# Layernorm statistics with tokens on the partitions, two layernorms in one call, and reordered loads

## The chip, the cores and the metric

The kernel runs on one core of a Trainium2 chip. The metric is the device time of one execution in microseconds (us). Engines are named as in the profile: PE is TensorE (PEld its weight loads), DVE is VectorE, ACT is ScalarE, POOL is GpSimd, SP is SyncE, which issues most DMAs.

## The reference

```python
def _A_ref(q, k, v, shift_k, ssm_k, ssm_D):      # q = layernorm(x), S = 2048 tokens, D = 512
    k_pad = jnp.pad(k, ((0, 0), (ks - 1, 0), (0, 0)))
    for t in range(ks):                          # ks = 4
        k_shift = k_shift + k_pad[:, t:t + S, :] * shift_k[:, ks - 1 - t][None, None, :]
    kv = k_shift * v
    kv_f = rfft(kv padded to 2 * S);  kf_f = rfft(ssm_k padded to 2 * S)
    y = irfft(kv_f * kf_f)[:S] + kv * ssm_D
    return q * y

def _B_ref(x, w1, w2, w3, w4):
    h = _gelu(_layernorm(x) @ w1)
    # four groups of channels, shifted by +1, -1, +2, -2 tokens
    hs = jnp.concatenate([g0, g1, g2, g3], axis=-1) @ w2
    x1 = x + hs
    return x1 + _gelu(_layernorm(x1) @ w3) @ w4  # w3: 512 x 1792

x = A_q
h = x + _A_ref(_layernorm(x), A_k, A_v, A_shift_k, A_ssm_k, A_ssm_D)
return h + _B_ref(_layernorm(h), B_w1, B_w2, B_w3, B_w4)
```

## The kernel before

Activations lie transposed: channels on the 128 partitions, in 4 chunks, and the 2048 tokens along the free side, mostly worked on in 4 windows of 512 (a block is 128 tokens). A tile scheduler takes the program in the order in which it is written and sets the order within each engine by its own rules; each engine and each DMA queue then works through its list in order.

The stages:

- Start: constants. `bj` (L71 to L74) and `rv` feed the angles of the transforms; `ssk` (L79 to L81) holds the shift weights. `xT` is A_q, transposed by four DMAs on SP (L95). They wait for the scaling of `bj` (L74), since the space of a temporary pool above it is used again.
- `layernorm_feat(xT, qnT, "qn")` (L156). The helper (L116 to L154) squares the whole input (`sq`, L122) and then goes window by window: 8 matmuls of 512 columns with `ones_col` as the stationary operand make sums in one row of one partition (L127, L129); mean, variance, square root, reciprocal and `brow` are computed on that row of 512 (L136 to L142); two f32 matmuls spread the rows over 128 partitions (`psbc`, L145, L146); two ScalarE copies make `abc` and `bbc` (L149, L150); 8 VectorE steps apply them (L153, L154).
- K and V: `kT` by transposing DMAs on SP (L170), `vT` on ScalarE's queue (L172). VectorE makes the shifted sum `ksh` (L175, L177) and the product `kvTc` (L181) of each chunk; TensorE transposes it block by block (L184) into `kv_all`, copied out by ScalarE and VectorE in turn (L187, L189). `hf`, the long filter, comes by 16 transposing DMAs on SP (L192).
- The transforms: a forward one over 17 strips (L202 to L261) and an inverse one over 4 windows (L273 to L295), by matmuls with sines and cosines that `gen_trig` makes on VectorE and ScalarE. Its last steps write `hT` (L294).
- `layernorm_feat(hT, hnT, "hn")` (L319), and `layernorm_feat(hnT, hnnT, "hnn")` (L331), which normalizes the result once more; mixer with `w1` and `w2` (L335 to L352), whose result is `x1T`.
- `layernorm_feat(x1T, ln1T, "ln1")` (L357); the last two matmuls with `w3` and `w4` and a gelu between them (L365 to L390). The weights `w3` and `w1` are loaded on SP's queue, `w4` and `w2` on ScalarE's.

`gelu_psum` (L298 to L308) starts with a ScalarE copy out of PSUM into `xs` (L300).

## Time and profile before

| | us |
|---|---|
| median of five runs | 839.98 (836.65 to 840.39) |
| profiled execution, its own time | 835.66 |
| its span | 833.9 |
| PE busy | 611.9 (73%) |
| DVE busy | 585.6 (70%) |
| ACT busy | 384.8 (46%) |
| PE weight loads busy | 249.9 (30%) |

The span runs from the first to the last instruction of the profiled execution; its own time lies 1.8 us above it. Busy shares are means over stages that are limited by different engines, so the sections below go by stage. In the profile's rows `L122` is line 122 of the kernel, `out<-in` names the tiles, `x4` counts instructions, and a bracket gives the idle time before a row and what released it.

### The profile page before, as it was taken

Reading aid. Unit: us, or ns where it says so; the run is one execution under the profiler, and the core shown is the slowest. Engines: PE = TensorE matmul, PEld = TensorE weight load, DVE = VectorE, ACT = ScalarE, POOL = GpSimd, SP = SyncE. Lnnn points to the kernel's source line nnn. Section 1 sums busy time; section 2 is a strip of 40 time slices with the busy share of each in tenths; the row PEclk is TensorE's granted clock in tenths of the full one; section 3 lists DMA queues with packets and bytes.
Section 4 is the critical chain, followed back from the end, with each engine's and each line's share of the span. In section 5 each row is a group of like instructions: output and inputs, shape, how many; then the busy total and the mean of one; then the engine's idle time right before and its main releaser. Section 6 shows DMA issues by size and latency. Waiting matters only on the chain.

```text
span 833.9 us, 6601 instructions
## 1 busy us (share of the span) xinstructions
PE 611.9 (73%) x2434; PEld 249.9 (30%) x2480; DVE 585.6 (70%) x882; ACT 384.8 (46%) x470; POOL 3.8 (0%) x10
## 2 busy tenths in 40 slices
PE   1550248999999999928999985657457456889885
PEld 0110113444444444403444431111123112334332
DVE  3886694747767666189999828978557894767665
ACT  0110136365564646258787721101392116786771
POOL 1000000000000000000000000000000000000000
PEclk9855558999999999978999995555699758999998
DMA  5006530000000000000000005010000000000000
GB/s 101 0 0 125 105 73 0 1 1 1 0 1 1 1 0 1 1 1 1 0 1 1 1 0 176 0 51 0 0 1 1 0 0 1 0 26 26 0 26 25
DMA packets 39921, 15.62 MB, mean 19 GB/s; under 512 B 34513, under 2 KB 39378, under 8 KB 39890
## 3 DMA queue, kind: packets, MB, share of 16 engines
q1 hardware_dynamic: 29234, 10.76, 5.4%
q10 hardware_dynamic: 10656, 4.46, 2.1%
q8 instruction: 19, 0.31, 0.2%
q14 instruction: 12, 0.10, 0.0%
HBM read 4.72 MB, written 2.10 MB: 8 GB/s over the span
## 4 chain that ended last, share of the span: by engine, by line
PE 52%; DVE 26%; ACT 13%; DMA 4%; issue 2%; SPq 1%; POOL 0%; ACTq 0%; DVEq 0%; POOLq 0%
PE yps L283 7%; PE yps L285 6%; PE ghi L222 6%; PE ghr L220 6%; DVE rows L141 6%; PE aki L221 6%; PE akr L219 6%; ACT xs L300 4%; PE po L378 4%; DVE u L305 3%; PE psbc L146 3%; DVE sq L122 2%; ACT u L302 2%; DMA kT<-in_A_k_dram 2%; ACT sg L307 2%
## 5 line engine op out<-in xcount | busy, mean ns | idle before, releaser
L283 PE MATMUL yps<-ics,Qr 128*128 128x512 bf16 x256 | 98.4, 384 | 18.6 <-ACT ics L114 17.8
L108 DVE TENSOR_TENSOR e<-bj,rv 128x2048 f32<-128x2048 f32 (+2 forms) x34 | 75.7, 2226 | 47.8 <-ACT cs L114 43.2
L222 PE MATMUL ghi<-hf,ss 128*128 128x512 bf16 x256 | 98.0, 383 | 0.7 <-issue 0.2
L220 PE MATMUL ghr<-hf,cs 128*128 128x512 bf16 x256 | 97.0, 379 | 0.5
L221 PE MATMUL aki<-kv_all,ss 128*128 128x512 bf16 x245 | 93.8, 383 | 1.3 <-ACT kv_all L187 1.3
L285 PE MATMUL yps<-iss,Qi 128*128 128x512 bf16 x245 | 93.9, 383 | 0.0
L219 PE MATMUL akr<-kv_all,cs 128*128 128x512 bf16 x246 | 93.3, 379 | 0.4 <-ACT cs L114 0.4
L113 ACT ACTIVATE e<-t 128x2048 f32<-128x2048 f32 (+2 forms) x34 | 63.0, 1852 | 49.2 <-DVE t L111 48.8
L378 PE MATMUL po<-g_sb,w_sb 128*128 128x512 bf16 x217 | 62.3, 385 | 23.8 <-DVE g_sb L308 21.8
L111 DVE TENSOR_TENSOR t<-e,t 128x2048 f32<-128x2048 f32 (+2 forms) x34 | 75.8, 2228 | 1.0
L145 PE MATMUL psbc<-rows,ones_row 1*128 1x512 f32 x32 | 28.4, 983 | 49.8 <-DVE rows L141 49.8
L141 DVE RECIPROCAL rows<-rows 1x512 f32<-1x512 f32 x16 | 53.4, 3335 | 5.0 <-ACT rows L140 5.0
L371 PE MATMUL pg<-ln1T,w_sb 128*128 128x512 bf16 x220 | 55.6, 387 | 1.6 <-ACT bbc L150 1.2
L140 ACT ACTIVATE rows<-rows,eps_t 1x512 f32<-1x512 f32 x16 | 11.5, 719 | 97.2 <-DVE rows L139 97.2
L307 ACT ACTIVATE sg<-u 128x512 bf16<-128x512 bf16 x72 | 44.9, 628 | 17.9 <-DVE u L305 16.7
L184 PE MATMUL pt<-ident,kvTc 128*128 128x128 bf16 x64 | 14.4, 269 | 50.5 <-DVE kvTc L181 24.1
L112 ACT ACTIVATE ss<-t 128x2048 bf16<-128x2048 f32 (+1 forms) x17 | 31.1, 1831 | 37.7 <-DVE t L111 37.6
L129 PE MATMUL stt<-sq,ones_col 128*1 128x512 bf16 x64 | 34.8, 582 | 16.7 <-DVE sq L122 16.7
L303 DVE TENSOR_SCALAR u<-u 128x512 bf16<-128x512 bf16 x72 | 20.5, 290 | 37.2 <-ACT u L302 36.2
L302 ACT ACTIVATE u<-xs 128x512 bf16<-128x512 bf16 x72 | 42.0, 626 | 0.3
L109 DVE TENSOR_SCALAR t<-e 128x2048 f32<-128x2048 f32 (+2 forms) x34 | 40.6, 1194 | 1.9
L114 ACT ACTIVATE ics<-e,halfpi 128x2048 bf16<-128x2048 f32 x16 | 32.0, 2002 | 20.8 <-PE yps L283 20.7
(108 smaller groups left out, 909.5 us busy)
## 6 DMA issues: line engine op xcount, KB each, us to landing
out_dram<-osb SPq DMA_DIRECT2D x16, 128.0 KB, 1.8
w_sb<-in_B_w_dram ACTq DMA_DIRECT2D x1, 1792.0 KB, 12.6
w_sb<-in_B_w_dram SPq DMA_DIRECT2D x1, 1792.0 KB, 8.7
w_sb<-in_B_w_dram ACTq DMA_DIRECT2D x1, 512.0 KB, 5.5
w_sb<-in_B_w_dram SPq DMA_DIRECT2D x1, 512.0 KB
hf<-in_A_ssm_k_dram SPq DMA_TRANSPOSE x16, 2.8
xT<-in_A_q_dram SPq DMA_TRANSPOSE x4, 5.1
kT<-in_A_k_dram SPq DMA_TRANSPOSE x4, 4.1
```

Of the source, the lines that this page charges most:

```text
L108: nc.vector.tensor_tensor(out=ev, in0=bj_b, in1=rv_b, op=MUL)
L111: nc.vector.tensor_tensor(out=tv, in0=ev, in1=tv, op=SUB)
L113: nc.scalar.activation(ev, tv, ACT.Abs)
L141: nc.vector.reciprocal(rstd, varr)
L219: nc.tensor.matmul(akr[:], lhsT=lhs_c, rhs=kv_all[:, b, :], start=st, stop=sp)
L220: nc.tensor.matmul(ghr[:], lhsT=lhs_c, rhs=hf[:, b, :], start=st, stop=sp)
L221: nc.tensor.matmul(aki[:], lhsT=lhs_s, rhs=kv_all[:, b, :], start=st, stop=sp)
L222: nc.tensor.matmul(ghi[:], lhsT=lhs_s, rhs=hf[:, b, :], start=st, stop=sp)
L283: nc.tensor.matmul(yps[:, c, :], lhsT=Qr[:, q, c * P:(c + 1) * P], rhs=ics[:, qi, :], start=(q == 0), stop=False)
L285: nc.tensor.matmul(yps[:, c, :], lhsT=Qi[:, q, c * P:(c + 1) * P], rhs=iss[:, qi, :], start=False, stop=False)
L307: nc.scalar.activation(sg[:], u[:], ACT.Sigmoid)
L378: nc.tensor.matmul(po[:], lhsT=w4_sb[:, k2, m * P:(m + 1) * P], rhs=g_sb[:, k2, :], start=(k2 == 0), stop=(k2 == FC - 1))
```

## The change

The helper gets its statistics in another layout. For each of 16 blocks and 4 chunks, the 128x128 block of the input, and that of its squares, is loaded as the stationary operand and multiplied by `ones_col`, one column. The sums of a token then stand on the token's partition, in `pst`, 128 partitions x 16 blocks x 2. The steps from mean to `brow` are done once, on 128x16 elements. To spread `rstd` and `brow` over the channels again, each block's column is multiplied into the identity (`dga`, `dgb`, 128x128, VectorE) and `ones_pp`, a 128x128 tile of ones, times that diagonal gives the broadcast in `psbc`. The copies and the apply steps stay.

With `yt2` the helper also makes the second normalization: from the variance of the first it works out the factor `ratio`, and `hnnT` is `hnT` times it. The call for "hnn" goes. For "ln1" the squares are made in four windows.

Loads: the `xT` DMAs come first on SP, ahead of `ssk_bf` and `Dvec`, and their tiles are placed before the temporary pool. `vT` moves to SP, alternating with `kT`; `w4` and `w2` move to SP too.

```diff
+    ones_pp = const.tile([P, P], BF16)
+    nc.gpsimd.memset(ones_pp[:], 1.0)
...
+    for c in range(DC):
+        nc.sync.dma_start_transpose(xT[:, c, :], A_q[0, :, c * P:(c + 1) * P])
     with ExitStack() as ctmp_ctx:
...
     nc.sync.dma_start(ssk_bf[:], A_shift_k.rearrange("(c p) j -> p c j", p=P))
     nc.vector.tensor_copy(ssk[:], ssk_bf[:])
     nc.sync.dma_start(Dvec[:], A_ssm_D[None, :])
...
-    for c in range(DC):
-        nc.sync.dma_start_transpose(xT[:, c, :], A_q[0, :, c * P:(c + 1) * P])
...
-    def layernorm_feat(xt, yt, name):
+    def layernorm_feat(xt, yt, name, yt2=None):
...
+            if name != "ln1":
+                nc.vector.tensor_tensor(out=sq[:], in0=xt[:], in1=xt[:], op=MUL)
+            else:
+                for w in range(NW):
+                    ws = slice(w * 512, (w + 1) * 512)
+                    nc.vector.tensor_tensor(out=sq[:, :, ws], in0=xt[:, :, ws], in1=xt[:, :, ws], op=MUL)
+            pst = lps.tile([P, NB, 2], F32, tag="pst", bufs=1)
+            for blk in range(NB):
+                lo, hi = blk * P, (blk + 1) * P
                 for c in range(DC):
-                    nc.tensor.matmul(stt[:, 0:512], lhsT=ones_col[:, :], rhs=xt[:, c, lo:hi],
+                    nc.tensor.matmul(pst[:, blk, 0:1], lhsT=xt[:, c, lo:hi], rhs=ones_col[:, :],
                                      start=(c == 0), stop=(c == DC - 1))
-                    nc.tensor.matmul(stt[:, 512:1024], lhsT=ones_col[:, :], rhs=sq[:, c, lo:hi],
+                for c in range(DC):
+                    nc.tensor.matmul(pst[:, blk, 1:2], lhsT=sq[:, c, lo:hi], rhs=ones_col[:, :],
                                      start=(c == 0), stop=(c == DC - 1))
...
+            nc.scalar.mul(stat[:], pst[:], 1.0 / D)
+            mean = stat[:, :, 0]
+            ex2 = stat[:, :, 1]
...
+            nc.vector.tensor_tensor(out=varr[:], in0=mean, in1=mean, op=MUL)
+            nc.vector.tensor_tensor(out=varr[:], in0=ex2, in1=varr[:], op=SUB)
...
+            nc.scalar.activation(den[:], varr[:], ACT.Sqrt, bias=eps_t[:], scale=1.0)
...
+            nc.vector.reciprocal(rstd[:], den[:])
...
+            nc.vector.scalar_tensor_tensor(out=brow[:], in0=mean, scalar=-1.0, in1=rstd[:],
+                                           op0=MUL, op1=MUL)
+            scales = [(rstd, brow, yt)]
+            if yt2 is not None:
...
+                nc.vector.tensor_scalar(out=den2[:], in0=varr[:], scalar1=1.0 + 1e-5,
+                                        scalar2=1e-10, op0=MUL, op1=ADD)
+                nc.scalar.activation(den2[:], den2[:], ACT.Sqrt)
...
+                nc.vector.reciprocal(rstd2[:], den2[:])
...
+                nc.vector.tensor_tensor(out=ratio[:], in0=den[:], in1=rstd2[:], op=MUL)
+                scales.append((ratio, None, yt2))
+            for (acol, bcol, ydst) in scales:
+                for w in range(NW):
+                    psbc = lps.tile([P, 1024], F32, tag="psbc")
+                    for j in range(4):
+                        blk = 4 * w + j
+                        dga = lp.tile([P, P], BF16, tag="dga", bufs=4)
+                        nc.vector.tensor_scalar_mul(dga[:], ident[:], acol[:, blk:blk + 1])
...
+                        nc.tensor.matmul(psbc[:, j * P:(j + 1) * P], lhsT=ones_pp[:, :],
+                                         rhs=dga[:], start=True, stop=True)
...
+                    nc.scalar.copy(abc[:], psbc[:, 0:512])
+                    lo, hi = w * 512, (w + 1) * 512
+                    if bcol is None:
+                        for c in range(DC):
+                            nc.vector.tensor_tensor(out=ydst[:, c, lo:hi], in0=yt[:, c, lo:hi],
+                                                    in1=abc[:], op=MUL)
+                        continue
...
-            for c in range(DC):
-                nc.scalar.dma_start_transpose(vT[:, c, :], A_v[0, :, c * P:(c + 1) * P])
+                nc.sync.dma_start_transpose(vT[:, c, :], A_v[0, :, c * P:(c + 1) * P])
...
-        nc.scalar.dma_start(w4_sb[:], B_w4.rearrange("(k p) o -> p k o", p=P))
-
-        layernorm_feat(hT, hnT, "hn")
+        nc.sync.dma_start(w4_sb[:], B_w4.rearrange("(k p) o -> p k o", p=P))
...
+            layernorm_feat(hT, hnT, "hn", yt2=hnnT)
...
-            nc.scalar.dma_start(w2_sb[:], B_w2.rearrange("(k p) o -> p k o", p=P))
+            nc.sync.dma_start(w2_sb[:], B_w2.rearrange("(k p) o -> p k o", p=P))
...
-            layernorm_feat(hnT, hnnT, "hnn")
```

SP's queue at the start of the program, before (what a row waits for stands in brackets, as semaphores of engines and DMAs):

```order
L79 DMA ssk_bf<-in_A_shift_k_dram 128x4x4
L84 DMA Dvec<-in_A_ssm_D_dram 1x512
L95 DMA_TRANSPOSE xT<-in_A_q_dram 128x2048 [waits DVE_49]
L95 DMA_TRANSPOSE xT<-in_A_q_dram 128x2048 x3
L170 DMA_TRANSPOSE kT<-in_A_k_dram 128x2048 [waits PE_49,Activation_49]
```

and now:

```order
L83 DMA_TRANSPOSE xT<-in_A_q_dram 128x2048 x4
L93 DMA ssk_bf<-in_A_shift_k_dram 128x4x4
L96 DMA Dvec<-in_A_ssm_D_dram 1x512
L209 DMA_TRANSPOSE kT<-in_A_k_dram 128x2048
L210 DMA_TRANSPOSE vT<-in_A_v_dram 128x2048
L209 DMA_TRANSPOSE kT<-in_A_k_dram 128x2048 [waits DMAHW0_49]
```

The transposes of A_q have moved to the head of the queue and have no wait; K no longer waits for TensorE and ScalarE, and V stands between its pieces. The later waits of K and V are for older DMAs.

VectorE in the first layernorm, before:

```order
L122 TENSOR_TENSOR sq<-xT 128x8192
L136 TENSOR_SCALAR rows<-stt 1x512
L138 TENSOR_TENSOR rows<-rows 1x512
L137 TENSOR_SCALAR rows<-stt 1x512
L139 TENSOR_TENSOR rows<-rows 1x512
L136 TENSOR_SCALAR rows<-stt 1x512
L137 TENSOR_SCALAR rows<-stt 1x512
L141 RECIPROCAL rows<-rows 1x512
```

and now (`ksh` is the shifted sum of K):

```order
L126 TENSOR_TENSOR sq<-xT 128x8192
L213 TENSOR_SCALAR ksh<-kT,ssk 128x2048 x2
L215 SCALAR_TENSOR_TENSOR ksh<-kT,ssk,ksh 128x2047
L145 TENSOR_TENSOR varr<-stat 128x16
L215 SCALAR_TENSOR_TENSOR ksh<-kT,ssk,ksh 128x2047
L146 TENSOR_TENSOR varr<-stat,varr 128x16
L215 SCALAR_TENSOR_TENSOR ksh<-kT,ssk,ksh 128x2046
L150 RECIPROCAL rstd<-den 128x16
L215 SCALAR_TENSOR_TENSOR ksh<-kT,ssk,ksh 128x2045
L152 SCALAR_TENSOR_TENSOR brow<-stat,rstd 128x16
```

The rows of 1x512 have gone, and steps of the shift of K, which stood behind the whole layernorm, stand between the 128x16 steps.

VectorE at the end of the layernorms ahead of the mixer, before:

```order
L139 TENSOR_TENSOR rows<-rows 1x512
L141 RECIPROCAL rows<-rows 1x512
L142 SCALAR_TENSOR_TENSOR rows<-rows 1x512
L153 TENSOR_TENSOR tn<-hnT,abc 128x512 x2
L154 TENSOR_TENSOR hnnT<-tn,bbc 128x512 x2
```

and now:

```order
L185 TENSOR_TENSOR hnnT<-hnT,abc 128x512 x4
L171 TENSOR_SCALAR dga<-ident,ratio 128x128 x9
L185 TENSOR_TENSOR hnnT<-hnT,abc 128x512 x8
L171 TENSOR_SCALAR dga<-ident,ratio 128x128
L185 TENSOR_TENSOR hnnT<-hnT,abc 128x512 x4
```

The second normalization has no statistics of its own; its 16 multiplies stand directly behind the first one, with the diagonals of `ratio` between them.

## Rows read from the trace of the kernel before

**Rows 1.** Windows by stage: stretch, length, busy us (count) of each engine, PEclk, DMA share, GB/s.
```profile
core 0: us, PE busy (x) PEld busy (x) DVE busy (x) ACT busy (x) POOL busy (x), PEclk, DMA share, GB/s
0.00:118.10 118.10, 37.13 (x95) 11.49 (x96) 81.85 (x109) 14.31 (x36) 3.63 (x8) 0.66 0.35 70
118.10:499.30 381.20, 350.43 (x1573) 156.48 (x1604) 262.55 (x275) 222.90 (x178) 0.00 (x0) 0.96 0.00 1
499.30:598.90 99.60, 57.51 (x99) 15.49 (x99) 81.53 (x114) 15.39 (x25) 0.14 (x2) 0.55 0.15 48
645.10:694.40 49.30, 27.65 (x53) 7.56 (x54) 40.73 (x57) 8.21 (x13) 0.00 (x0) 0.63 0.00 0
```

**Rows 2.** Groups of instructions: count | busy us, mean ns | idle before, releaser.
```profile
L141 DVE RECIPROCAL rows<-rows 1x512 f32<-1x512 f32 x16 | 53.4, 3335 | 5.0 <-ACT rows L140 5.0
```

**Rows 3.** Transposes on TensorE: one timeline row (start, us), then groups with means.
```profile
725.44 0.27 PE L386 MATMUL pt<-ident,fb 128*128 128x128 bf16 x2
...
L386 PE MATMUL pt<-ident,fb 128*128 128x128 bf16 x64 | 10.9, 222 | 1.8 <-DVE fb L383 1.5 <-DVE osb L387 0.3
L184 PE MATMUL pt<-ident,kvTc 128*128 128x128 bf16 x64 | 14.4, 269 | 50.5 <-DVE kvTc L181 24.1 <-ACT kv_all L187 15.9 <-DVE kv_all L189 10.2
L184 PEld LDWEIGHTS <-kvTc 128*128 128x128 bf16 x64 | 6.6, 107 | 59.3 <-issue 32.7 <-DVE kvTc L181 25.7
```

**Rows 4.** Timeline of SP's queue and of VectorE at the start: start, us, instruction, idle before.
```profile
0.73 0.46 SPq L79 DMA_DIRECT2D ssk_bf<-in_A_shift_k_dram  x1
4.43 10.17 SPq L95 DMA_TRANSPOSE xT<-in_A_q_dram  x4
...
2.73 0.17 DVE L81 CAST ssk<-ssk_bf 128x16 f32<-128x16 bf16 x1 [1.70 <-DMA ssk_bf<-in_A_shift_k_dram]
4.31 1.23 DVE L74 TENSOR_SCALAR bj<-bj 128x2056 f32<-128x2056 f32 x1
16.86 4.42 DVE L122 TENSOR_TENSOR sq<-xT 128x8192 bf16<-128x8192 bf16 x1 [11.32 <-DMA xT<-in_A_q_dram]
```

**Rows 5.** Groups of VectorE: a small step, and a step of the shift of K.
```profile
L109 DVE TENSOR_SCALAR t<-e 128x16 f32<-128x16 f32 x1 | 0.2, 174 | 0.0
...
L177 DVE SCALAR_TENSOR_TENSOR ksh<-kT,ssk,ksh 128x2047 bf16<-128x2047 bf16 x4 | 9.4, 2344 | 0.0
```

**Rows 6.** Timeline of VectorE at the landmarks.
```profile
63.37 0.76 DVE L153 TENSOR_TENSOR tn<-xT,abc 128x512 bf16<-128x512 bf16 x2 [2.83 <-ACT abc L149]
...
65.39 0.75 DVE L154 TENSOR_TENSOR qnT<-tn,bbc 128x512 bf16<-128x512 bf16 x2
...
96.06 1.22 DVE L181 TENSOR_TENSOR kvTc<-ksh,vT 128x2048 bf16<-128x2048 bf16 x1
97.19 0.35 DVE L189 COPY kv_all<-pt 128x128 bf16<-128x128 bf16 x2
...
498.01 1.28 DVE L294 TENSOR_TENSOR hT<-ty,xT 128x512 bf16<-128x512 f32 x2
...
644.35 0.69 DVE L352 TENSOR_TENSOR x1T<-pw,hnT 128x512 bf16<-128x512 f32 x1 [0.25 <-PE pw L350]
```

**Rows 7.** Timeline of SP's queue, and TensorE's first matmul of the transform.
```profile
62.76 27.75 SPq L170 DMA_TRANSPOSE kT<-in_A_k_dram  x4
97.09 21.14 SPq L192 DMA_TRANSPOSE hf<-in_A_ssm_k_dram  x16
...
128.85 0.59 PE L221 MATMUL aki<-kv_all,ss 128*128 128x512 bf16 x1 [1.29 <-ACT kv_all L187]
```

**Rows 8.** DMA issues: count, KB each, us from issue to landing.
```profile
w_sb<-in_B_w_dram ACTq DMA_DIRECT2D x1, 1792.0 KB, 12.6
...
hf<-in_A_ssm_k_dram SPq DMA_TRANSPOSE x16, 2.8
```

**Rows 9.** Timeline of ScalarE: inputs of the two gelus, and a table load.
```profile
600.25 0.58 ACT L300 CAST xs<-pw 128x512 bf16<-128x512 f32 x1 [0.65 <-PE pw L340]
...
601.90 1.28 ACT L307 ACT_TABLE_LOAD   x1
...
695.75 0.58 ACT L300 CAST xs<-pg 128x512 bf16<-128x512 f32 x1 [0.65 <-PE pg L371]
```

More of the change, by code (lines that the diff above doesn't have):

```diff
@@ L68 @@
     rv = const.tile([P, 20], F32)
+    ssk_bf = const.tile([P, DC, 4], BF16)
+    ssk = const.tile([P, DC, 4], F32)
+    Dvec = const.tile([1, D], BF16)
+    Qr = const.tile([P, 17, D], BF16)
+    Qi = const.tile([P, 16, D], BF16)
+    hT = const.tile([P, DC, S], BF16)
+    pI_ctx = ExitStack()
+    pI = pI_ctx.enter_context(tc.tile_pool(name="pI", bufs=1))
+    xT = pI.tile([P, DC, S], BF16)
+    qnT = pI.tile([P, DC, S], BF16)
+    for c in range(DC):
+        nc.sync.dma_start_transpose(xT[:, c, :], A_q[0, :, c * P:(c + 1) * P])
     with ExitStack() as ctmp_ctx:
@@ L139, in layernorm_feat @@
-                nc.vector.tensor_tensor(out=varr, in0=varr, in1=rstd, op=SUB)
-                nc.scalar.activation(varr, varr, ACT.Sqrt, bias=eps_t[0:1, :], scale=1.0)
-                nc.vector.reciprocal(rstd, varr)
-                nc.vector.scalar_tensor_tensor(out=brow, in0=mean, scalar=-1.0,
-                                               in1=rstd, op0=MUL, op1=MUL)
-                psbc = lps.tile([P, 1024], F32, tag="psbc")
-                nc.tensor.matmul(psbc[:, 0:512], lhsT=ones_row32[:, :], rhs=rstd, start=True, stop=True)
@@ L146, in layernorm_feat @@
-                nc.tensor.matmul(psbc[:, 512:1024], lhsT=ones_row32[:, :], rhs=brow, start=True, stop=True)
-                abc = lp.tile([P, 512], BF16, tag="abc")
-                bbc = lp.tile([P, 512], BF16, tag="bbc")
-                nc.scalar.copy(abc[:], psbc[:, 0:512])
-                nc.scalar.copy(bbc[:], psbc[:, 512:1024])
-                for c in range(DC):
-                    tn = lp.tile([P, 512], BF16, tag="tn")
-                    nc.vector.tensor_tensor(out=tn[:], in0=xt[:, c, lo:hi], in1=abc[:], op=MUL)
-                    nc.vector.tensor_tensor(out=yt[:, c, lo:hi], in0=tn[:], in1=bbc[:], op=ADD)
+            stat = lq.tile([P, NB, 2], F32, tag="stat")
@@ L170 @@
                 nc.sync.dma_start_transpose(kT[:, c, :], A_k[0, :, c * P:(c + 1) * P])
-            for c in range(DC):
-                nc.scalar.dma_start_transpose(vT[:, c, :], A_v[0, :, c * P:(c + 1) * P])
+                nc.sync.dma_start_transpose(vT[:, c, :], A_v[0, :, c * P:(c + 1) * P])
             for c in range(DC):
```

48 lines of the change are left out of this document (23 added, 25 removed).

## Prediction, made before the changed kernel had run

> **What bounds the kernel now.** I read the windows by stage first [rows 1]. In the two transforms (118.1 to 499.3) TensorE sets the pace: 350 of 381 us busy at a granted clock of 0.96. In the three stretches that hold a layernorm (0 to 118.1, 499.3 to 598.9, 645.1 to 694.4) no engine is full: VectorE leads with 82 of 118, 82 of 100 and 41 of 49 us, and TensorE is at clocks of 0.55 to 0.66. Those are chains of short dependent steps on several engines. The groups of instructions name the dearest: the reciprocal of 512 numbers on one partition, 3.335 us, sixteen times [rows 2]. So I price the change as three new chains, each from the moment its input is ready to a landmark that both programs share, and leave the rest as it is. The start and end of each old chain is read in the timelines [rows 4, 6, 9].
>
> **Price of the new statistics.** Each layernorm now needs 128 pairs of one weight load (128x128) and one matmul with a single moving column; before has no such pair. Nearest are the transposes, pairs of a load and a matmul of 128 columns. Two of them with a mean of 0.222 us took 0.27 together near the end, so the second started 0.05 after the first [rows 3]. One column leaves less to do than 128, so it can go below: low end 0.03, my estimate, about half of that. High end 0.135, half of the 0.27, as if the two had not overlapped at all. I forecast 0.065, near the row in which pairs really follow each other. Four of the 128 don't wait for the last squares, so 124 x 0.065 = 8.1 us a layernorm; 372 pairs in three.
> One rule speaks against the change. A load's record lasts 107 ns in the slow first part [rows 3]. The Trainium skill, page "TensorE: Matmul & The Clock Gate", section "LDWEIGHTS (loading the stationary operand)", has a load take its columns over 1.2 GHz, 107 ns for 128 of them, however few rows it has. The length agrees with the trace; that loads follow each other no closer is what the 0.05 contradicts. By the rule the statistics of one layernorm would be 13.3 us; rival A is that case.
>
> **Front, from 0 to the second kvTc.** SP issues xT at 0.73, where the shift weights went, instead of 4.43: 3.7 earlier, since nothing of bj is waited for now [rows 4]. The last xT had landed when sq began at 16.86, so it lands near 13.1. The shift weights now queue behind xT and land about 0.4 later, 13.5; their cast (0.17) and the scaling of bj (1.23) stand ahead of sq on VectorE [rows 4], so sq (4.42) runs from about 14.8 to 19.2. POOL's new memset goes ahead of the making of bj, which was ready to be scaled at 4.31, far ahead of xT: hidden. While the statistics run to 19.2 + 8.1 = 27.3, VectorE does the first three steps of ksh. The column pair is copied by 27.9. From there VectorE's order counts: two 128x16 steps of 0.17 [rows 5], three steps of ksh of 2.3 between them [rows 5], a reciprocal of 128x16 at 0.25 (its bounds: 0.17 as the other 128x16 step, and 0.8, a quarter of the 1x512 one), one step more of 0.18 and eight diagonals. A diagonal is a 128x128 step; two 128x128 copies took 0.35 together [rows 6], and I take 0.14 to 0.16 each, bounds 0.11 and 0.21. Sum 8.9: 36.8. One matmul and two copies are about 1.0: 37.8. The apply of one window is 2.7, from 63.37 to 66.14 [rows 6]; four are 10.8, the next diagonals stand twice uncovered ahead of a window (1.3 each), and kvTc of the first chunk (1.2) stands between: qnT ends at 52.4. Two steps of ksh, five copies and kvTc of the second chunk: 58.6. Before, that one ended at 96.06 + 1.22 = 97.3 [rows 6]. Gain 38.7, of which I count **38**. From there VectorE has the same list in both programs through the first angles of the transform, so its start moves by as much.
> Cover for the loads: kT and vT now alternate on SP's queue without a wait for the layernorm. Four xT took 10.17 us of it [rows 4], 2.5 each; eight from 12 are through by 33. Even at 6.9 each, a quarter of the 27.75 that four kT took with waits in it [rows 7], the fourth is there by 41, ahead of 57. hf waits for the last qnT, 52.4; 21.1 us of issues [rows 7] and 2.8 to landing [rows 8] end at 77, and the first matmul of the transform goes from 128.85 [rows 7] to 91. The slack is 14 us; beyond it each us of a later hf costs one.
>
> **Layernorm of h and the second one on its result.** The last hT ended at 498.01 + 1.28 = 499.3 [rows 6], T0. sq undivided 4.43 with 0.1 ahead; statistics 8.1; copy 0.45, table load 1.28 [rows 9], square root 0.3, three 128x16 steps 0.7, eight diagonals 1.3, matmul and copies 1.0, together 5.0: 17.6. (The small ScalarE steps lie between the 0.17 of a 128x16 step [rows 5] and the 0.58 of a 128x512 copy [rows 9].) Four windows 10.8 and three sets of diagonals 3.8: 32.2. The second one is a product with a ratio: 16 multiplies of 0.34 (0.68 from one pair's start to the next, [rows 6]) are 5.4, ten diagonals not yet done 1.4, matmul and copy 1.2: 40.2. The second gelu input follows two groups of matmuls from cold, 2.8 later, at T0 + 43.0; before it started at 600.25 [rows 9], T0 + 101.0. **Gain 58.**
> w4, w1 and w2 now go through SP's queue behind w3, whose issue still waits for hT. By the slowest landing, 12.6 [rows 8], w3 and w4 one after the other take 25, and w1 3.6, a quarter and a bit of that, by its size: 29 after T0. It is asked for at 40. Hidden by 11 us.
>
> **Layernorm of x1.** The last x1T ended at 644.35 + 0.69 = 645.04 [rows 6], T1. The squares go in four pieces; only the last, a quarter of 4.4 plus 0.1, stands behind it: 1.3. Statistics 8.1; the same small steps 4.6: 14.0. Windows as above, 14.6: 28.6. The first matmuls behind it need only the first window, so the second gelu input comes at + 29.2; before at 695.75 [rows 9], + 50.7. **Gain 21.5.**
>
> **Rest.** In the transforms, the gelu stages and the output each engine keeps its list; 0. ScalarE no longer issues vT, w4 and w2; it stood idle there.
>
> **Sum.** 38 + 58 + 21.5 = 117.5. The profiled run took 835.66 (span 833.9), which makes 718.2; the median of the runs, 839.98, is 4.3 above it. Prediction **722**.
>
> **Rivals.**
> A. Loads do not overlap: a pair takes the 0.107 of a load's record [rows 3]. For it: the layernorm stretches have the low clock [rows 1], and the 0.05 was seen at the high one. Against: the two overlapping transposes. 372 x 0.042 = 15.6 more: 738.
> B. The slower side: every pair runs alone, the matmul after its load and the next load after the matmul: 0.107 + 0.269 [rows 3] + 0.05 of hand-over (the closest two starts) = 0.43. 372 x 0.365 = 136 lost on TensorE against 117.5 won: 722 + 136 = 858. It decides from 0.38 a pair, where 372 x 0.315 eats the gain. Against: no row has neighbours that far apart while nothing is waited for, and 0.269 is for 128 columns.
> C. One queue makes something late: hf past its 14 us of slack, or w1 behind two large weights past its 11. A transfer a third slower than the slowest row brings a miss of some 3 to 13 us: 725 to 735.
> D. One column costs less than I allow, 0.03: 372 x 0.035 = 13 less, 709.
> That the change does not do what it says is excluded for the sixteen reciprocals: they are gone from VectorE's list, and so is what follows them on one partition.
>
> **How the numbers follow.** Forecast 0.63, A 0.2, D 0.1, C 0.05, B 0.02. The range takes in D, C and A and the ends of the pair's price: 0.03 gives 709, 0.135 gives 722 + 26 = 748; the 112 diagonals at +- 0.05 are +- 5.6, of which some 4 at the low end. So 705 to 750; B and the outermost tails are left out. About 0.3% is what a measurement of this kernel can tell from no change; every case but B is faster by much more: faster 0.97, same 0.01, slower 0.02.
>
> **What would show it.** In the changed profile no 1x512 step on VectorE; 128 one-column matmuls a layernorm, over about 8 us after sq's end (13 is A, over 40 is B); kvTc of the second chunk ending near 58.6, and the transform's first matmul near 91 with hf landed; second gelu inputs at + 43 and + 29 from the ends of hT and x1T. I am wrong if the transforms themselves lengthen, if VectorE stands waiting for K or V before qnT is done, or if the diagonals take turns with the matmuls and copies they feed instead of running ahead of them.

## The result, and the profile after

The changed kernel takes **711.64 us** (median of 8 runs, 710.96 to 713.04), the kernel before 838.64 (median of 15 runs, 834.7 to 841.51). The ratio is 0.849, with a 95% interval of 0.847 to 0.851. The forecast of 722 was 10.4 too high, inside its range of 705 to 750. The profiled run of after took 712.75, its span is 711.0.

The windows of the kernel after; the columns are those of [rows 1]. The first row ends with the first layernorm, the other four are cut where [rows 1] is cut: at the first angles of the transform, the last hT, the first gelu input of the mixer, and from the last x1T to the first gelu input behind it.

```profile
core 0: us, PE busy (x) PEld busy (x) DVE busy (x) ACT busy (x) POOL busy (x), PEclk, DMA share, GB/s
0.00:50.40 50.40, 10.18 (x162) 7.23 (x163) 35.39 (x85) 7.37 (x12) 2.73 (x9) 1.00 0.72 125
0.00:77.70 77.70, 21.25 (x211) 12.32 (x212) 62.05 (x123) 14.00 (x37) 2.73 (x9) 1.00 0.59 108
77.70:462.40 384.70, 350.42 (x1570) 155.51 (x1600) 258.07 (x273) 223.37 (x176) 0.00 (x0) 0.98 0.00 1
462.40:498.80 36.40, 13.70 (x176) 8.79 (x178) 29.85 (x105) 8.43 (x16) 0.14 (x2) 0.50 0.39 130
545.50:570.90 25.40, 11.73 (x165) 7.66 (x166) 21.60 (x72) 6.08 (x11) 0.00 (x0) 0.57 0.01 1
```

Against [rows 1]: the stretch of the two layernorms between the transforms and the mixer, 99.6 us with 81.5 of VectorE, is now 36.4 with 29.9; the front went from 118.1 to 77.7, the layernorm of x1 from 49.3 to 25.4. VectorE still leads in all three, but with less to do. The transforms have the same 350 us of TensorE and are nevertheless longer, 384.7 for 381.2; the ledger below, which starts at their first matmul, has more of it.

The timeline rows of after at the landmarks that answer to [rows 4, 6, 7, 9] (start, us, engine, line, instruction, idle before):

```profile
0.73 10.57 SPq L83 DMA_TRANSPOSE xT<-in_A_q_dram  x4
15.13 4.42 DVE L126 TENSOR_TENSOR sq<-xT 128x8192 bf16<-128x8192 bf16 x1
55.34 1.21 DVE L219 TENSOR_TENSOR kvTc<-ksh,vT 128x2048 bf16<-128x2048 bf16 x1
86.28 0.59 PE L259 MATMUL aki<-kv_all,ss 128*128 128x512 bf16 x1 [1.56 <-ACT kv_all L225]
461.12 1.28 DVE L332 TENSOR_TENSOR hT<-ty,xT 128x512 bf16<-128x512 f32 x2
500.49 0.58 ACT L338 CAST xs<-pw 128x512 bf16<-128x512 f32 x1 [1.08 <-PE pw L376]
544.81 0.69 DVE L388 TENSOR_TENSOR x1T<-pw,hnT 128x512 bf16<-128x512 f32 x1 [0.25 <-PE pw L386]
572.18 0.58 ACT L338 CAST xs<-pg 128x512 bf16<-128x512 f32 x1 [0.65 <-PE pg L407]
```

From these rows and those of before, the ledger of the two spans. T0 is the end of the last hT (499.29 before, 462.40 after), T1 that of the last x1T (645.04 and 545.50):

| Stretch | before, us | after, us | gain forecast | gain |
|---|---|---|---|---|
| 0 to the transform's first matmul | 128.85 | 86.28 | 38 | 42.6 |
| first matmul to T0 (both transforms) | 370.4 | 376.1 | 0 | **-5.7** |
| T0 to the second gelu input of the mixer | 101.0 | 38.1 | 58 | 62.9 |
| from there to T1 | 44.8 | 45.0 | 0 | -0.2 |
| T1 to the second gelu input of the FFN | 50.7 | 26.7 | 21.5 | 24.0 |
| from there to the end | 138.2 | 138.8 | 0 | -0.7 |
| sum | 833.9 | 711.0 | 117.5 | 122.9 |

Three terms came out larger than forecast by 12.0 us together, one that was set at nothing lost 5.7. The first part is the price of the new statistics. In the layernorm of h (timeline of after, a few rows of VectorE, TensorE and ScalarE):

```profile
462.44 4.42 DVE L126 TENSOR_TENSOR sq<-hT 128x8192 bf16<-128x8192 bf16 x1
...
467.05 0.24 PE L135 MATMUL pst<-ones_col,hT 128*128 128x1 bf16 x4
467.16 0.24 PE L138 MATMUL pst<-ones_col,sq 128*128 128x1 bf16 x4
467.26 0.24 PE L135 MATMUL pst<-ones_col,hT 128*128 128x1 bf16 x4
...
470.42 0.20 ACT L141 ACTIVATE stat<-pst 128x32 f32<-128x32 f32 x1 [24.04 <-PE pst L138]
```

Groups of four pairs start about 0.107 us apart, so a pair of a load and a matmul costs **0.0267 us**. From the end of sq (466.86) to the copy of the statistics pass 3.6 us where 8.1 and the start of that copy were forecast. That is rival D's price, not the 0.065 chosen and not rival A's 0.107.

### The profile page after: what moved, and what is told of

Read it like the earlier page. It is cut to its first block, busy times and chain, and to the rows that moved or that the text cites. A ratio compares the mean times of both kernels' runs of the same rounds, so it can differ in the third digit from the quotient of the medians.

```text
span 711.0 us, 7192 instructions
## 1 busy us (share of the span) xinstructions
PE 541.3 (76%) x2738; PEld 244.4 (34%) x2784; DVE 490.5 (69%) x899; ACT 375.9 (53%) x458; POOL 2.9 (0%) x11
## 4 chain that ended last, share of the span: by engine, by line
PE 38%; DVE 33%; ACT 22%; issue 3%; SPq 2%; DMA 1%; ACTq 0%; DVEq 0%
PE yps L321 8%; PE yps L323 8%; PE po L414 5%; ACT xs L338 4%; DVE t L114 4%; DVE e L111 4%; ACT e L116 3%; ACT ss L115 3%; DVE ksh L215 3%; ACT cs L117 3%; DVE u L343 3%; PE ghi L260 3%; PE aki L259 2%; ACT u L340 2%; PE ghr L258 2%
## 5 line engine op out<-in xcount | busy, mean ns | idle before, releaser
L111 DVE TENSOR_TENSOR e<-bj,rv 128x2048 f32<-128x2048 f32 (+2 forms) x34 | 75.7, 2226 | 92.3 <-ACT cs L117 88.0
L114 DVE TENSOR_TENSOR t<-e,t 128x2048 f32<-128x2048 f32 (+2 forms) x34 | 75.7, 2225 | 0.7
L175 PE MATMUL psbc<-dga,ones_pp 128*128 128x128 bf16 x64 | 15.8, 270 | 46.1 <-DVE dga L171 45.4
L341 DVE TENSOR_SCALAR u<-u 128x512 bf16<-128x512 bf16 x72 | 20.5, 290 | 38.1 <-ACT u L340 37.1
L117 ACT ACTIVATE ics<-e,halfpi 128x2048 bf16<-128x2048 f32 x16 | 32.0, 2003 | 20.4 <-PE yps L321 20.3
L323 PEld LDWEIGHTS <-Qi 128*128 128x128 bf16 x256 | 25.3, 99 | 48.0 <-issue 18.7
L112 DVE TENSOR_SCALAR t<-e 128x2048 f32<-128x2048 f32 (+2 forms) x34 | 40.5, 1192 | 1.6
L338 ACT CAST xs<-pg 128x512 bf16<-128x512 f32 x56 | 32.3, 578 | 14.4 <-PE pg L407 8.8
L414 PEld LDWEIGHTS <-w_sb 128*128 128x128 bf16 x224 | 21.5, 99 | 51.0 <-issue 33.9
L257 PEld LDWEIGHTS <-cs 128*128 128x128 bf16 x256 | 25.0, 98 | 38.2 <-ACT cs L117 9.3
```

The lines of the kernel that those rows point to most:

```text
L111: nc.vector.tensor_tensor(out=ev, in0=bj_b, in1=rv_b, op=MUL)
L114: nc.vector.tensor_tensor(out=tv, in0=ev, in1=tv, op=SUB)
L257: nc.tensor.matmul(akr[:], lhsT=lhs_c, rhs=kv_all[:, b, :], start=st, stop=sp)
L323: nc.tensor.matmul(yps[:, c, :], lhsT=Qi[:, q, c * P:(c + 1) * P], rhs=iss[:, qi, :], start=False, stop=False)
L338: nc.scalar.copy(xs[:], psrc)
L414: nc.tensor.matmul(po[:], lhsT=w4_sb[:, k2, m * P:(m + 1) * P], rhs=g_sb[:, k2, :], start=(k2 == 0), stop=(k2 == FC - 1))
```

## The experiments

All times are medians; "after" stands for 711.64. The kernel before, measured beside each of these kernels, had medians of 836.9 to 839.5, so a difference of 2 us is believed here only where a trace shows the same.

**The loads alone, and the layernorm alone.** The first kernel is the one before with the changed order and queues of the loads; the second has the changed layernorm with the loads as they were.

```diff
+    for c in range(DC):
+        nc.sync.dma_start_transpose(xT[:, c, :], A_q[0, :, c * P:(c + 1) * P])
     with ExitStack() as ctmp_ctx:
...
-            for c in range(DC):
-                nc.scalar.dma_start_transpose(vT[:, c, :], A_v[0, :, c * P:(c + 1) * P])
+                nc.sync.dma_start_transpose(vT[:, c, :], A_v[0, :, c * P:(c + 1) * P])
```

> Edit: the kernel before with only the load moves (xT first on SP, vT, w4 and w2 on SP); the layernorms are the old ones. Theory 1, the gain is the layernorms': K still waits for the pools of the old layernorm, so only xT's 1.7 us (16.9 to 15.1 at the start of sq) and a shorter K and V load (before: 8 transposes from 62.8 to about 95; eight of 2.6 in a row would be 21) are won, and the forward transform loses some 5 us because ScalarE's list in it is like that of the changed kernel: 824 to 836. Theory 2, the early loads carry the front's gain of 40: 800 or less.

> Edit: the changed kernel with the loads as before (xT behind the shift weights and after bj, vT, w4 and w2 on ScalarE's queue). Theory 1, the layernorms carry the gain: the two later ones give 87 us as in the changed kernel, the front is some 10 us longer since SP's list now has the four K transposes ahead of xT, and the forward transform is 5 to 8 us shorter since ScalarE's list in it takes the next strip's Abs ahead of the four copies from the second strip on: 706 to 722. Theory 2, the loads carry the front's gain: 740 to 750.

Measured: the loads alone 827.51 (ratio 0.987, interval 0.983 to 0.990), as the first theory had it. The layernorm alone took 732.55, between its two theories and in neither. Where the loads alone stop is shown by the waits of SP's queue in that kernel (who waited for whom: us in total, times, longest):

```profile
SPq L170 <- PE psbc L146: 48.6, 1, 48.6
```

The issue of K waits 48.6 us for a matmul of the old layernorm (L146), so K comes no earlier than the old chain lets it. With the layernorm alone, the scheduler put the four kT ahead of xT on SP's queue. Its timelines of SP and VectorE:

```profile
4.96 27.65 SPq L209 DMA_TRANSPOSE kT<-in_A_k_dram  x4
32.71 10.24 SPq L97 DMA_TRANSPOSE xT<-in_A_q_dram  x4
...
45.88 4.42 DVE L126 TENSOR_TENSOR sq<-xT 128x8192 bf16<-128x8192 bf16 x1 [14.00 <-DMA xT<-in_A_q_dram]
```

sq starts at 45.88 instead of 15.13. The first copy of akr out of PSUM (akr is one of the four sums that a strip of the forward transform makes, so its copies count the strips) stands at 144.06 before, 128.81 with the loads alone (15.3 won), 127.23 with the layernorm alone (16.8 won) and 102.41 with both (41.7 won). The two parts win 9.6 us more in the front together than the sum of each. The rows above fit this reading: the layernorm frees what K's issue waited for, and the loads deliver what the shorter layernorm then asks for.

**V's loads back on ScalarE's queue.** The changed kernel with this alone undone:

```diff
-                nc.sync.dma_start_transpose(vT[:, c, :], A_v[0, :, c * P:(c + 1) * P])
+            for c in range(DC):
+                nc.scalar.dma_start_transpose(vT[:, c, :], A_v[0, :, c * P:(c + 1) * P])
```

> Edit: the changed kernel with vT back on ScalarE's queue. Theory 1: two queues of transposes do not run beside each other (the kernel with the old loads took 27.7 us for K and V together on two queues, one queue with 2.6 each takes 21), so the second K, for which VectorE now waits 2.6 us, comes some 2 us later and the loads end 6 us later, of which VectorE notices little: 712 to 715. Theory 2: without V ahead of it the second K lands 2.6 us earlier: 708.5 to 710.

Measured: 731.7 (730.69 to 733.86), 20 us slower than after. Both theories missed it. Rows of this kernel's timeline, of the two queues and of VectorE:

```profile
0.72 26.52 ACTq L211 DMA_TRANSPOSE vT<-in_A_v_dram  x4
5.00 26.71 SPq L83 DMA_TRANSPOSE xT<-in_A_q_dram  x4
...
36.84 4.42 DVE L126 TENSOR_TENSOR sq<-xT 128x8192 bf16<-128x8192 bf16 x1
```

and of the waits of its SP queue (who waited for whom: us in total, times, longest):

```profile
SPq L83 <- DMA vT<-in_A_v_dram: 23.8, 4, 6.9
```

Each transposing load on SP waits for the end of one on ScalarE's queue, up to 6.9 us, and by their starts the two queues take turns: V at 0.72, xT at 5.00, V at 9.24, xT at 13.21 and so on, some 4.1 us apart. That is the time of one load of V from issue to landing (4.0 to 4.3). The four xT take 26.71 instead of 10.57 and are through at 31.71 instead of 11.30. By the 2.6 of one queue, four loads of V ahead of the last xT would be some 10.5 of these 20.4 us even there (an estimate); the taking of turns is the other half. This is also what the 27.75 for four kT in [rows 7] was: in before, V stood on ScalarE's queue too. The Trainium skill, page "DMA: Bandwidth & Descriptors", section "Rules for kernel authors", has it that DMA transposes on different queues must be put one behind the other, because two in flight corrupt each other. The waits of this trace agree. The 20 us are their cost together with that of V's standing ahead.

**Without the shared second layernorm.**

```diff
-            layernorm_feat(hT, hnT, "hn", yt2=hnnT)
+            layernorm_feat(hT, hnT, "hn")
...
+            layernorm_feat(hnT, hnnT, "hnn")
```

> Edit: the changed kernel with the second normalization as a layernorm call of its own (own squares and statistics, no ratio). By the rows of the changed kernel a layernorm takes 4.4 for sq, 3.5 for the statistics, 4.6 for the small steps and the first diagonals, 15 for the windows, 27.5; the fused one takes 8.2 behind the first: 18 to 20 us more, 730. If instead the fusion is most of the gain of 63 in that stretch, 40 or more: over 750.

Measured: 729.05 (727.88 to 730.8), 17.4 more than after, about as expected. In its timeline the second layernorm squares its own input from 490.26 and copies its own statistics at 498.30. Of the 62.9 won behind T0, some 17 belong to taking the second layernorm from the first one's statistics, the rest to the shorter chain.

**Twice the pairs.** Each statistics matmul is done twice, with the same result.

```diff
-            for blk in range(NB):
+            for blk in [b_ for b_ in range(NB) for _ in range(2)]:
```

> Edit: the changed kernel with every block's statistics made twice, 256 pairs of weight load and one-column matmul a layernorm. By the changed trace a pair costs 0.027 (four in 0.107): 128 more are 3.4 us, all of it on the path in the layernorm of h, about half in that of x1 where the pairs run beside the squares, about 1 us in the first where VectorE has the steps of the K shift meanwhile: 5 to 8 us more, 717 to 720. If pairs cost what a load's record lasts, 0.107, three times 13.7: 740 or more; if the matmuls run beside VectorE's work in all three: 712.

Measured: 717.52 (716.51 to 718.21), as expected, though not by the additions expected. In the layernorm of h, from sq's end (463.37) to the copy of the statistics, 9.7 us pass instead of 3.6:

```profile
458.95 4.42 DVE L126 TENSOR_TENSOR sq<-hT 128x8192 bf16<-128x8192 bf16 x1
...
471.51 0.27 PE L138 MATMUL pst<-ones_col,sq 128*128 128x1 bf16 x4 [2.59 <-issue]
...
473.10 0.20 ACT L141 ACTIVATE stat<-pst 128x32 f32<-128x32 f32 x1 [30.21 <-PE pst L138]
```

The 252 pairs that follow sq at 0.0267 make 6.7; a gap of 2.59 in which TensorE waited for nothing that the profile shows makes the rest. What that gap is stays open. The forward transform of this kernel was 5 us shorter than after's (first to last copy of akr 207.87 against 213.0), which hid about as much of the cost, and pointed to the question of the transforms, below.

**Squares of x1 in one piece.**

```diff
-            if name != "ln1":
+            if True:
```

> Edit: the changed kernel with the squares of x1 in one step instead of four. Theory 1, the four pieces win only the overlap of the pairs with the squares, since VectorE's list has all four behind the last x1T: sq 4.43 for 4.62 and statistics 3.5 for 1.1, 2.2 us more, 713.5 to 714.5. Theory 2, of the prediction, three pieces are hidden ahead of the last x1T: 5 to 6 us more, 717.

Measured: 713.85 (712.78 to 714.34), 2.2 more than after: the first theory. In its trace T1 to the second gelu input of the FFN takes 29.3 instead of 26.7. The prediction had thought that the first three of the four pieces run ahead of the last x1T. In after (timeline of VectorE and ScalarE) they don't:

```profile
545.42 4.62 DVE L130 TENSOR_TENSOR sq<-x1T 128x2048 bf16<-128x2048 bf16 x4
551.16 0.20 ACT L141 ACTIVATE stat<-pst 128x32 f32<-128x32 f32 x1 [19.63 <-PE pst L138]
```

All four pieces stand behind the last x1T. The split pays because TensorE's pairs overlap the later pieces: the copy of the statistics comes 1.1 after the last piece, against 3.6 after an undivided sq.

**Why the transforms got longer.** The loss of 5.7 lies in the forward transform: from the first matmul to the first copy of akr 15.2 before and 16.1 after, from the first to the last copy of akr (15 strips) 207.9 and 213.0, the rest 147.4 and 147.0. The two kernels do the same work there in a different order on ScalarE and on VectorE. ScalarE makes three things for each strip: the sine (ss), the absolute value of the angles (e<-t, "the Abs") and from it the cosine (cs). From its compiled lists, in a later strip, before:

```
L112 ACTIVATE ss<-t 128x2048
L114 ACTIVATE cs<-e,halfpi 128x2048
L113 ACTIVATE e<-t 128x2048
L227 CAST acr<-akr 128x512
L228 CAST aci<-aki 128x512
L229 CAST gcr<-ghr 128x512
L230 CAST gci<-ghi 128x512
```

and after, where the same Abs (e<-t) stands ahead of the cosine of its own strip, not ahead of the four copies:

```
L115 ACTIVATE ss<-t 128x2048
L116 ACTIVATE e<-t 128x2048
L117 ACTIVATE cs<-e,halfpi 128x2048
L265 CAST acr<-akr 128x512
L266 CAST aci<-aki 128x512
L267 CAST gcr<-ghr 128x512
L268 CAST gci<-ghi 128x512
```

Before has the first order from the copies of its seventh strip on, after has the second one in all its full strips. VectorE makes the angles in three steps, L111, L112 and L114 in after. In after's first eleven strips its list has the second and the third of them behind the products of the strip before (behind all but the last of them); in before only the first two strips have that. What this makes of the two engines shows in after's timeline of one strip:

```profile
168.44 1.91 ACT L115 ACTIVATE ss<-t 128x2048 bf16<-128x2048 f32 x1 [6.71 <-DVE t L114]
170.26 1.89 ACT L116 ACTIVATE e<-t 128x2048 f32<-128x2048 f32 x1
172.19 2.00 ACT L117 ACTIVATE cs<-e,halfpi 128x2048 bf16<-128x2048 f32 x1
...
174.22 2.29 DVE L111 TENSOR_TENSOR e<-bj,rv 128x2048 f32<-128x2048 f32 x1 [5.81 <-ACT cs L117]
176.43 0.42 DVE L271 TENSOR_TENSOR p<-acr,gcr 128x512 bf16<-128x512 bf16 x1
...
180.51 2.28 DVE L114 TENSOR_TENSOR t<-e,t 128x2048 f32<-128x2048 f32 x1
```

There is one buffer for e, so VectorE's next angles wait for the cosine that reads e (5.81), and ScalarE's next sine waits for those angles (6.71). The two take turns: sine, Abs and cosine 5.8, angles with the products in between 8.6, together the period of 14.39, which ten periods in a row have. TensorE's own pace is 13.81, 64 matmuls of 0.216, so that TensorE comes to wait for the cosine, 0.62 us behind the one shown. Before has one such period; nine more of them at 0.58 are the 5.2 by which the 15 strips are longer.

Is it the place of the Abs or that of the angle steps? Both kernels have strips that tell. In before, from 200 us on, the Abs still stands behind the sine, but the angle steps come in a row, ahead of the products:

```profile
200.39 2.29 DVE L108 TENSOR_TENSOR e<-bj,rv 128x2048 f32<-128x2048 f32 x1 [5.21 <-ACT cs L114]
202.72 1.23 DVE L109 TENSOR_SCALAR t<-e 128x2048 f32<-128x2048 f32 x1
203.98 2.29 DVE L111 TENSOR_TENSOR t<-e,t 128x2048 f32<-128x2048 f32 x1
206.30 1.91 ACT L112 ACTIVATE ss<-t 128x2048 bf16<-128x2048 f32 x1 [4.01 <-DVE t L111]
208.12 1.89 ACT L113 ACTIVATE e<-t 128x2048 f32<-128x2048 f32 x1
210.04 2.00 ACT L114 ACTIVATE cs<-e,halfpi 128x2048 bf16<-128x2048 f32 x1
212.08 2.29 DVE L108 TENSOR_TENSOR e<-bj,rv 128x2048 f32<-128x2048 f32 x1 [2.74 <-ACT cs L114]
```

The round from one first angle step to the next is 11.7 there, well under TensorE's 13.81, with the Abs where it stands in after. After's last strips go the same way: its copies follow each other at 13.78, 13.91 and 13.53 while the angle steps move ahead of the products, without a change in ScalarE's order. So what makes 14.39 is the products between the angle steps, in a round that the single buffer closes.

Three kernels tried to undo it. In the first, e and t have two buffers; in the second, Abs writes a tile of its own:

```diff
-        tmpf = pa_ctx.enter_context(tc.tile_pool(name="tmpf", bufs=1))
+        tmpf = pa_ctx.enter_context(tc.tile_pool(name="tmpf", bufs=2))
```

```diff
+        ab = pool.tile([P, gmax, cw], F32, tag="ga")
+        av = ab[0:np_, 0:g, :]
...
-        nc.scalar.activation(ev, tv, ACT.Abs)
-        nc.scalar.activation(out_cos, ev, ACT.Sin, bias=halfpi[0:np_, :], scale=-TWO_PI)
+        nc.scalar.activation(av, tv, ACT.Abs)
+        nc.scalar.activation(out_cos, av, ACT.Sin, bias=halfpi[0:np_, :], scale=-TWO_PI)
```

> Edit: the changed kernel with two buffers instead of one for the angle tiles e and t of the forward transform. Theory 1: the 5.7 us that the transforms lost lie in the forward one, where each strip takes 14.4 instead of 13.55 since the next strip's angles wait for the cosine of this one and ScalarE takes Abs behind it; with two buffers ScalarE's list takes Abs of the next strip ahead and a strip is bound by TensorE at 13.6: 15 strips x 0.6 to 0.85 = 9 to 13 us less, 699 to 703. Theory 2, TensorE itself is slower in the changed kernel (clock, or its operands' memory): no change, 711 to 712.

> Edit: the changed kernel with the absolute value of the angles written to a tile of its own instead of over e. Two angle buffers gave strips of 13.81 in the forward transform instead of 14.4, but VectorE then made both first strips' angles before the first sine and the first copy of the transform came 5.2 us later (107.6 instead of 102.4). Theory 1: what makes a strip 14.4 long is that VectorE's next e waits for the cosine that reads e; with Abs in its own tile e is free after VectorE's own step, the first strip stays where it is, and the strips are 13.8: 5 to 6 us less, 705 to 707. Theory 2: ScalarE's list with its chain of sine, Abs, cosine and four copies is the limit and a strip stays at 14.4: 711 to 712.

Measured: 712.78 (711.57 to 713.45) and 714.15 (713.95 to 716.02); neither is faster, both forecasts missed. In both the periods are 13.81 to 13.86 in every full strip, as the theory says, and the 5.8 are won there. The tile for Abs does so with VectorE's second and third angle steps still behind the products: it opens the round at the buffer instead, since the first step no longer waits for the cosine. But each of them moved other instructions too. With two buffers VectorE makes the angles of the first two strips in one go ahead of the first strip's sine (timeline of VectorE):

```profile
79.93 4.48 DVE L111 TENSOR_TENSOR e<-bj,rv 128x2048 f32<-128x2048 f32 x2
84.33 2.36 DVE L112 TENSOR_SCALAR t<-e 128x2048 f32<-128x2048 f32 x2
86.60 4.49 DVE L114 TENSOR_TENSOR t<-e,t 128x2048 f32<-128x2048 f32 x2
```

The first copy of akr moves from 102.41 to 107.63, and the gain is gone. With the tile for Abs it moves to 105.62, and the inverse part grows from 147.0 to 152.2, where TensorE waits 22.56 instead of 17.81 for the inverse transform's first angles. So the third kernel leaves the lists outside the forward transform as they are: the program writes the angles and the Abs of the strip after next ahead of the four copies, and from the copies of the fifth strip on ScalarE's list takes the order of before. On ScalarE only the Abs moves; on VectorE the three angle steps move with it.

```diff
+                    nxt = finish(ang, fchunks[n + 1][1])
+                    if n + 2 < len(fchunks):
+                        ang = angles(*fchunks[n + 2])
                     nc.scalar.copy(acr[:], akr[:])
```

(finish makes sine and cosine of a strip, angles its three VectorE steps and the Abs.)

> The changed kernel; in the loop of the forward transform the angles and the Abs of the strip after next are written ahead of the four PSUM copies of the present one. Of ScalarE's list in the transform only the place of the Abs changes: from the fifth strip or so it stands ahead of the four copies, as in the later strips of the kernel before; the last copies of K*V, the first strip, the inverse transform and all behind it keep their lists. Theory 1 (the place of the Abs is what cost the transforms 5.7 us): first copy of akr at 102.4 as now, periods of 14.4 for the first strips, one long one of some 17.8 at the switch, then 13.5 to 13.8; first to last copy 207 to 209 instead of 213.0; inverse part 147; the time 705 to 708. Theory 2 (the transforms are longer for another reason, as what the earlier start does to the first strips, and the list is only a companion of it): periods stay at 14.2 to 14.4 and the time at 711 to 713.

Measured: **707.25** (706.83 to 707.58), 4.4 less than after: the first theory. Its first copy of akr stands at 101.55, the first to the last take 207.1, with periods of 13.55 behind one long one of 16.69; the rest is 147.7. From the first matmul to T0 370.2 pass, where before has 370.4 and after 376.1. (1.5 of this is lost again in the mixer, 46.5 for 45.0; why was not looked into.) ScalarE's timeline of one strip:

```profile
184.82 1.91 ACT L253 ACTIVATE e<-t 128x2048 f32<-128x2048 f32 x1 [6.00 <-DVE t L252]
186.64 0.57 ACT L297 CAST acr<-akr 128x512 bf16<-128x512 f32 x1
...
188.53 1.94 ACT L258 ACTIVATE ss<-t 128x2048 bf16<-128x2048 f32 x1
190.34 2.02 ACT L259 ACTIVATE cs<-e,halfpi 128x2048 bf16<-128x2048 f32 x1
```

With the Abs ahead of the copies VectorE makes its angles without the products in between (the 6.00 ahead of the Abs), and the copies' round is 13.55. It can be shorter than TensorE's 13.81 because the copies catch up after the long period; over 15 strips all kernels without the ten long rounds take 207 to 208, TensorE's pace. That settles the 5.7 as the order of the two engines' lists. This kernel moved the Abs and the angle steps together; the strips above say that the angle steps are enough. The 0.9 ahead of the first copy is not explained by either.

**The second diagonal on ScalarE.** VectorE is the leader of the layernorms, ScalarE has room.

```diff
-                            nc.vector.tensor_scalar_mul(dgb[:], ident[:], bcol[:, blk:blk + 1])
+                            nc.scalar.mul(dgb[:], ident[:], bcol[:, blk:blk + 1])
```

> Edit: the changed kernel with the second diagonal of each block (dgb) made by ScalarE instead of VectorE. Theory 1, VectorE bounds the apply of the windows: a window is 2.7 of apply and 8 diagonals of 0.163; four fewer win 0.65 a window, 2.6 a layernorm, 7 to 8 in all; ScalarE's list in the forward transform has Abs ahead from the third strip on in this build, 4 to 5 more: 698 to 702. Theory 2, the diagonals' way through TensorE and ScalarE's copies bounds a window: the layernorms keep their length and only the transform wins: 706 to 708.

Measured: 699.25 (698.38 to 700.25), 12.4 less than after, as the first theory has it. Two rows of its timeline, VectorE's first windows in the layernorm of h:

```profile
468.92 0.76 DVE L192 TENSOR_TENSOR tn<-hT,abc 128x512 bf16<-128x512 bf16 x2
...
471.61 0.75 DVE L192 TENSOR_TENSOR tn<-hT,abc 128x512 bf16<-128x512 bf16 x2
```

These two windows follow each other at 2.7, with no diagonals between; in after they stand 4.07 apart (475.10 and 479.17). T0 to the second gelu input is 34.6 instead of 38.1, T1 to that of the FFN 23.3 instead of 26.7. About half of the gain is not the diagonals': this kernel's lists have no products between the angle steps (first to last copy 207.2, 5.8 less than after).

**The first strip's angles made while xT is awaited**, and then all of it together: early angles, the second diagonal on ScalarE, and all squares in four pieces.

```diff
+    cs0 = const.tile([P, NB, 128], BF16)
+    ss0 = const.tile([P, NB, 128], BF16)
+    z_last = gen_trig(z, 0, NB, 0, 128, ss0[:, :, :], cs0[:, :, :], NB)
...
-            gen_trig(tmpf, 0, NB, f0, cw, ss[:, :, :cw], cs[:, :, :cw], NB)
+            if f0 == 0:
+                cs, ss = cs0, ss0
+            else:
+                gen_trig(tmpf, 0, NB, f0, cw, ss[:, :, :cw], cs[:, :, :cw], NB)
```

> Edit: the changed kernel with the angles of the first strip (e, t, t on VectorE, sine, Abs, cosine on ScalarE) made at the start, while VectorE waits for xT, in tiles of their own; ordering edges put them ahead of the shift weights' cast and the squares, and the squares ahead of the K steps. Theory 1, the front is bound by VectorE's work after xT's landing: 5.8 us of it go (2.3 + 1.2 + 2.3) and both halves of the first strip are ready when the last block of kv_all is, so the first copy of the transform comes at 96 to 97 instead of 102.4; ScalarE's list takes Abs ahead from the second strip on, strips of 13.8 instead of 14.4 win 5 to 6 more: 699 to 703. Theory 2, the front waits for hf or the K loads: the first copy stays at 101 to 102 and only the strips win: 706.

> Edit: the changed kernel with all of these: the first strip's angles at the start, dgb on ScalarE, the squares of every layernorm in four pieces. If the gains add: 5.6 at the front, 5.5 in the strips, 7.5 from the diagonals, 2.3 from the statistics of the layernorm of h beside its squares, 21: 688 to 694. If the diagonals on ScalarE stand in the way of its copies: 696 or more.

Measured: 706.02 (705.47 to 707.15), at the smaller of the two gains expected, and **697.07** (696.32 to 697.89; ratio to before 0.829, interval 0.827 to 0.832), short of the 688 to 694 of adding gains. It lies in the range of the other theory, whose reason doesn't show: the windows of x1's layernorm have the diagonals' gain in full (23.3, as above). The early angles bring the first copy of akr forward by 0.85 only, to 101.56: VectorE's list now has the second strip's angles, 2.28 + 1.22 + 2.28 from 76.87 on, between the copies of kv_all that the first matmuls need (read from its timeline, not tested further). What it wins, 5.8 in the transform, it wins by the order of the lists (periods of 13.81 throughout). The kernel with everything has its first copy at 99.81, but its inverse part is 152.2 instead of 147.0. That is not the longer wait of the kernel with a tile for the Abs: here two of the four windows of the inverse transform take 31.0 instead of 28.7, and TensorE waits 2.9 for angles. Two pieces of the squares of h stand in them on VectorE, but a third stands in a window of 28.7, so the cause stays open. The pieces also bring the copy of the statistics of h to 2.5 behind T0, from 8.0, since three of the four run ahead of it. It beats both kernels, 14.6 us below after.

## Why the prediction was right, and where it was wrong

**Direction, place and mechanism were right.** What bound the kernel were the chains in the layernorm stretches. The gain came where it was forecast, 42.6, 62.9 and 24.0 for 38, 58 and 21.5, and VectorE still leads there. That the total came out only 10.4 off is luck in part: three terms were 12.0 too small, and the transforms' 5.7 went the other way.

**The step that failed: the transforms at 0.** "In the transforms, the gelu stages and the output each engine keeps its list" is not so. In the forward transform the lists of VectorE and ScalarE differ. After keeps the products between the angle steps for ten periods of 14.39, before for one, and that costs 5.2 of the 5.7. That the transforms lengthen was the first sign that the prediction named against itself. The orders were there to be read: [rows 1] only gave the average of a transform that in before starts in one order (14.13 and 14.38) and has left it by the third period.

**The term that was mis-sized: the pair**, 0.0267 for 0.065. In the layernorm of h the copy of the statistics came 8.0 after T0 where the steps of the prediction add up to 12.6. That is 4.6 of the 4.9 by which this term was larger. All that follows, small steps, windows, diagonals and the ratio, fits to 0.3: a diagonal takes 0.163 (the eight of the second window start from 477.79 to 478.93), at the edge of the 0.14 to 0.16 taken. Rival D, to which the prediction gave a chance of 0.1, was the case; A and B are out. The Trainium skill, page "TensorE: Matmul & The Clock Gate", section "LDWEIGHTS (loading the stationary operand)", has a load of 128 columns last 107 ns; taken as the spacing of loads, as in rival A, that makes an estimate of 13.3 for a layernorm's statistics. The 3.6 measured decides against it as a spacing. As the length of one load it is near: a row of after, the loads of sq in the layernorm of x1 (count: shortest, median and longest ns), has 96. They overlap:

```profile
L138 PEld LDWEIGHTS <-sq x64: 95/96/116, 546.7 to 550.8; 128*128 128x128 bf16 x64
```

**ln1**: two errors against each other. The squares end 4.5 behind T1 and not 1.3 (a quarter of 4.4 and 0.1 are 1.2, a slip of 0.1), and the pairs need 1.1 more and not 8.1. Together 3.7 were won at the copy of the statistics. 1.2 were lost again: the four windows took 15.1 for 14.6, and the second gelu input came 1.3 behind the last of them instead of 0.6.

**The front**: the cheap pairs could win little, because VectorE is its leader (35.4 of 50.4 us busy). The copy of the statistics was done at 23.4, 4.5 ahead of the forecast, but the step that reads it comes at 25.74, behind VectorE's steps on K, one of which had waited for its load:

```profile
22.81 0.75 DVE L213 TENSOR_SCALAR ksh<-kT,ssk 128x2048 bf16<-128x2048 bf16 x1 [2.59 <-DMA kT<-in_A_k_dram]
23.18 0.20 ACT L141 ACTIVATE stat<-pst 128x32 f32<-128x32 f32 x1 [17.28 <-PE pst L138]
25.74 0.17 DVE L145 TENSOR_TENSOR varr<-stat 128x16 f32<-128x16 f32 x1
```

That wait is one that the prediction named as a sign against itself; it cost little. kvTc of the second chunk ended at 56.55, forecast 58.6. Of the 4.6 more that the front won, 2.0 stand there, 0.7 are the rounding of 38.7 to 38, and 1.8 come behind it, where the start of the transform did not move "by as much": in before VectorE waited some 2 us there for the last transposes on TensorE. hf was issued from 50.53 to 71.2, ahead of the first matmul at 86.28, so rival C did not come. (The prediction's 77 for hf's landing adds up to 76.3; nothing hangs on it.)

**A right number with a reason missing: V's move to SP's queue.** It was costed as nothing on ScalarE and as 2.5 a load on SP, which is about what it took (2.2 to 3.2). That the alternative, V on the other queue and early, costs 20 us was not seen, though the 6.9 a load of [rows 7] stood in the text as a bound. In the kernel with the layernorm alone, V on ScalarE's queue and K ahead of xT, 24.8 of the front's gain are missing (127.23 against 102.41).

**The offset.** The forecast added 4.3 because the median of before lay so far above its profiled run. With more runs it lies 3.0 above, and after's median lies 1.1 below its own profiled run. The 4.3 and the 1.1 make 5.4; the ledger's 122.9 against 117.5 is another 5.4, and 0.5 went the other way when the forecast was rounded to 722.

## What to carry to other kernels

Statistics over the partition axis that end on one partition are dear because all that follows runs on one lane; with the data as the weights and a single column moving, they come out with one number in each lane, and a pair of a load and a matmul cost 0.027 us here. Before a stage is booked at nothing because its code is unchanged, compare what the scheduler laid out for it in both kernels, engine by engine: here a few steps of VectorE that moved behind others made ten strips 0.58 us longer each, and several of the experiments gained or lost as much by such a move as by what they were made for. Keep transposing loads on one queue, and look at what stands ahead of them there.
